# A Fourier mixing layer in front of a gated feed-forward: the 47-point transform first, the complex 64-point one second, data as matmul weights in the mixing

## The chip, the cores and the metric

The kernel runs on one core of a Trainium2 chip, in one launch. The metric is the device time of that launch in microseconds (us). The core's engines work beside each other: TensorE (PE, with its weight loads shown apart as PEld), VectorE (DVE), ScalarE (ACT), GpSimd (POOL), and SyncE (SP), which here only issues DMAs. Results of TensorE land in PSUM, everything else is in SBUF.

## The reference, cut to what matters

```
X  = np.fft.rfft(x, axis=1)                 # x: (8, 3008, 256), float32
Yr = Xr @ w_r - Xi @ w_i + b_r              # w_r, w_i: (256, 256)
Yi = Xr @ w_i + Xi @ w_r + b_i
Yr = sign(Yr) * max(|Yr| - 0.01, 0);  Yi likewise
y  = np.fft.irfft(Yr + 1j*Yi, n=3008, axis=1)
t  = y.reshape(24064, 256)
h  = t @ w_in                               # (256, 2048), float64
out = (h * cos(h)) @ w_out                  # (2048, 256), float64
```

The first six lines are called the Fourier part here, the last three the feed-forward.

## The kernel before

**The Fourier part.** 3008 = 64 * 47, and the two factors have no common divisor, so the 3008-point transform is a 64-point one along one index and a 47-point one along the other, with no twiddle factors between. It is done in three stages for each batch b, with a trip through DRAM (`scr1`, `scr2`) between them. `stage_a(b)` (lines 319 to 359) is the real 64-point transform: a fixed matrix is the weights, the data stream past it, 12 chunks of 512 columns. `stage_b(b)` (362 to 581) does four steps for 32 values of the first frequency, in four groups q of eight: `f2t1` is the 47-point transform with the data as weights, so that the result comes out with the 256 channels on the partitions; `wmix` multiplies by w_r, w_i and their sum, these as weights, and thresholds; `inverse` turns the result back with TensorE transposes (`t2`) and does the inverse 47-point transform (`idft`). `stage_c(b, t)` (586 to 645) is the inverse 64-point transform for block t of 512 tokens (six blocks t a batch, the last of 448), again with data as weights; it leaves the tokens as `xTh` and `xTl`, channels on partitions.

**The number format of the products.** Where accuracy needs it, a float32 operand is split into two float32r parts, high and low, and a product takes three matmuls (high*high, low*high, high*low). The high part is a cast, the low part a subtraction on POOL (`rest_pool`) or DVE (`rest`). For batch 0 the stages use plain float32 matmuls. The trace records a float32 matmul as two records: `f2t1` of batch 0 does four matmuls for a pair of values and shows eight.

**The feed-forward.** `moe_step(b, t, f, pull)` does one of 16 slices f of the inner 2048 for one block t: six matmuls into `ph`, then ACT and DVE make `u` = h cos h and its parts `gh`, `gl`; three slices later `second` adds six matmuls into the two `po` banks. All of these are float32r matmuls of 512 columns (448 in the last block).

**What sets the order.** In the opening, batch 0's `stage_a0` and `stage_b(0)` run with `stage_a(1)` woven in, and with them half of the splitting of w_in and w_out out of float64 (`split_f64`, sixteen pieces: eight of w_in, eight of w_out; DVE, ACT and POOL). Then the feed-forward of batch b runs block by block, and between its slices `pull` takes steps of the generator `ahead(b)`: `stage_c` of the next block, `stage_b(b+1)`, and `stage_a(b+2)` woven in. The number behind each `yield` is the cost by which `pull` meters these steps. The remaining eight pieces are split during batch 0's first block. Each engine then runs its own instructions strictly in the order in which they were laid down.

```
544            bo = stage_out("bo")[:96]
545            nc.scalar.copy(bo, p[:96])
...
547            nc.sync.dma_start(dst[:, s0:s0 + 2, :], bo.rearrange("p (s d) -> p s d", s=2))
```

Of the kernel before, what the change touches and what calls it, by code (L numbers as in the profile page):

```python
# [53 lines left out]
def _index():  # L54
    n1, n2 = np.arange(64), np.arange(48)
    return (47 * n1[None, :] + 64 * n2[:, None]) % N


def _constants():
    n1, s = np.arange(64), np.arange(32)  # L60
    ang = 2 * np.pi * (np.outer(n1, s) % 64) / 64
    f1 = np.zeros((2, 64, 2, 2, 32))
    ei = np.zeros((2, 2, 32, 2, 64))
    alt = (-1.0) ** n1
    for g in range(2):
        f1[g, :, 0, g, :] = np.cos(ang)
        f1[g, :, 1, g, :] = -np.sin(ang)
        f1[g, :, 1, g, 0] = alt
        ei[0, g, :, g, :] = np.cos(ang).T
        ei[1, g, :, g, :] = -np.sin(ang).T  # L70
        ei[1, g, 0, g, :] = alt

    f1 = f1.reshape(128, 4, 32).transpose(0, 2, 1).reshape(128, 128)
    ei = ei.reshape(128, 128) * (2.0 / N)
    crt = {(k % 64, k % 47): k for k in range(N)}
    th = 2 * np.pi * (np.outer(np.arange(47), np.arange(47)) % 47) / 47
    C, S = np.cos(th), np.sin(th)
    f2 = np.zeros((32, 2, 48, 2, 48))
    sig = np.ones((32, 48))
    for sl in range(1, 32):  # L80
        for k2 in range(47):
            sig[sl, k2] = 1 if crt[sl, k2] <= N // 2 else -1
        f2[sl, 0, :47, 0, :47] = C
        f2[sl, 1, :47, 0, :47] = S
        f2[sl, 0, :47, 1, :47] = -S * sig[sl, :47]
        f2[sl, 1, :47, 1, :47] = C * sig[sl, :47]
    i1 = np.zeros((2, 2, 48, 2, 48))
    i1[1, 0, :47, 0, :47] = C
    i1[1, 0, :47, 1, :47] = S
    i1[1, 1, :47, 0, :47] = -S  # L90
    i1[1, 1, :47, 1, :47] = C
    for r, k1 in ((0, 0), (1, 32)):
        for j in range(24):
            c = r * 24 + j
            sig[0, c] = 1 if crt[k1, j] <= N // 2 else -1
            f2[0, r, :47, 0, c] = C[:, j]
            f2[0, r, :47, 1, c] = -S[:, j] * sig[0, c]
            i1[0, 0, c, r, :47] = (0.5 if j == 0 else 1.0) * C[j]
            if j:
                i1[0, 1, c, r, :47] = -S[j]  # L100
    f2 = np.concatenate([f2, f2[:, :, :, :1] + f2[:, :, :, 1:]], 3)
    f2 = f2.reshape(32, 96, 144).transpose(1, 0, 2)

    i1 = i1.reshape(2, 96, 4, 24).transpose(1, 0, 3, 2).reshape(96, 2, 96)
    c_f1 = np.stack(_split(f1), 1)
    c_f3 = f2.astype(np.float32)
    c_f2 = np.concatenate(_split(f2[:, :, :96]), 2)
    c_i1 = np.stack(_split(i1), 1)
    c_ei = np.concatenate(_split(ei), 1)
    c_sig = np.concatenate([np.ones((48, 32)), sig.T]).astype(np.float32)  # L110
    c_ff = np.concatenate([f1, ei], 1).astype(np.float32)
    c_if = i1.astype(np.float32)
    return [np.ascontiguousarray(a) for a in (c_f1, c_f2, c_i1, c_ei, c_sig, c_f3, c_ff, c_if)]
# [3 lines left out]
def tile_body(ctx: ExitStack, tc, x, w_r, w_i, b_r, b_i, w_in, w_out,  # L117
              c_f1, c_f2, c_i1, c_ei, c_sig, c_f3, c_ff, c_if, out):
# [9 lines left out]

    ff = cp.tile([128, 256], F32, name="ff")
    nc.gpsimd.dma_start(ff, c_ff)  # L130
    f1 = cp.tile([128, 2, 128], F32R, name="f1")
    ident = cp.tile([128, 128], F32, name="ident")
    make_identity(nc, ident)
    i1 = cp.tile([96, 2, 2, 96], F32R, name="i1")
    ei = cp.tile([128, 256], F32R, name="ei")
    sig = cp.tile([96, 32], F32, name="sig")


    bb = cp.tile([128, 2, 2], F32, name="bb")
    blo = cp.tile([128, 2, 2], F32, name="blo")  # L140
    bhi = cp.tile([128, 2, 2], F32, name="bhi")
    bhn = cp.tile([128, 2, 2], F32, name="bhn")

    def load_constants():
        with nc.allow_non_contiguous_dma(reason="bias"):
            for r, bsrc in enumerate((b_r, b_i)):
                nc.gpsimd.dma_start(bb[:, r, :], bsrc.rearrange("(c p) -> p c", p=128))
        nc.gpsimd.dma_start(sig, c_sig)
        nc.gpsimd.dma_start(fi[0], c_if)

    def load_split_constants():
        nc.gpsimd.dma_start(f1, c_f1)
        nc.gpsimd.dma_start(i1, c_i1)
        nc.gpsimd.dma_start(ei, c_ei)

    def bounds():
        nc.vector.tensor_scalar(out=blo, in0=bb, scalar1=-1.0, scalar2=-LAM, op0=ALU.mult, op1=ALU.add)
        nc.vector.tensor_scalar(out=bhi, in0=bb, scalar1=-1.0, scalar2=LAM, op0=ALU.mult, op1=ALU.add)
        nc.vector.tensor_scalar(out=bhn, in0=bhi, scalar1=-1.0, scalar2=None, op0=ALU.mult)

# [5 lines left out]
    def split_w(hi, lo, src):  # L166
        nc.vector.tensor_copy(hi, src)
        nc.vector.tensor_tensor(out=lo, in0=src, in1=hi.bitcast(F32), op=ALU.subtract)

    fi, ws, f0, a0 = {}, {}, {}, {}  # L170

    def load_fourier_w():
        wr, wi, wc = (pool["pro"].tile([128, 512], F32, tag=n, name=n, bufs=1) for n in ("wr", "wi", "wc"))
        ws.update(enumerate((wr, wc, wi)))
# [3 lines left out]
    def sum_fourier_w():  # L178
        wr, wc, wi = (ws[j] for j in range(3))
        nc.vector.tensor_tensor(out=wc, in0=wi, in1=wr, op=ALU.subtract)  # L180
        nc.vector.tensor_tensor(out=wi, in0=wi, in1=wr, op=ALU.add)

    def split_fourier_w():
        for j, w in ws.items():
            split_w(wf[:, j, 0].rearrange("p c e -> p (c e)"), wf[:, j, 1].rearrange("p c e -> p (c e)"), w)
# [10 lines left out]
    def split_f64(hi, lo, raw):  # L196
# [43 lines left out]
    mm = nc.tensor.matmul  # L240

    def rest_pool(lo, x, hi):
        return nc.gpsimd.tensor_tensor(out=lo, in0=x, in1=hi.bitcast(F32), op=ALU.subtract)  # L243

    def rest(lo, x, hi):
        return nc.vector.tensor_tensor(out=lo, in0=x, in1=hi.bitcast(F32), op=ALU.subtract)  # L246

    scr1, scr2 = {}, {}

# [10 lines left out]
    def stage_in(name):  # L260
        return wk.tile([128, 512], F32, tag="xt", name=name, bufs=4)

    def stage_out(name):
        return wk.tile([128, 512], F32, tag="ao", name=name, bufs=3)

    def beside(*gens):
        gens = list(gens)
        while gens:
            for g in list(gens):
                c = next(g, None)  # L270
# [554 lines left out]
```

## Time and profile before

| | |
|---|---|
| median of 3 runs | 2763.29 us (2761.89 to 2765.01) |
| span of the profiled execution | 2764.1 us |
| PE busy | 2726.7 us, 99% of the span, 13422 matmul records |
| DVE busy | 2099.5 us, 76% |
| ACT busy | 1783.9 us, 65% |
| POOL busy | 1193.0 us, 43% |
| DMA | 174.54 MB, 63 GB/s in the mean |

The profiled execution's span lies within the three runs. A matmul's busy time in the trace is longer than the time that it holds TensorE up, since the next one starts before it has ended: a 128x512 matmul shows 0.39 us, and the next starts 0.23 us after it. So what a matmul costs is read from start to start.

### The profile page before, as it was taken

Reading aid. Unit: us, or ns where it says so; the run is one execution under the profiler, and the core shown is the slowest. Engines: PE = TensorE matmul, PEld = TensorE weight load, DVE = VectorE, ACT = ScalarE, POOL = GpSimd, SP = SyncE. Lnnn points to the kernel's source line nnn. Section 1 sums busy time; section 2 is a strip of 40 time slices with the busy share of each in tenths; the row PEclk is TensorE's granted clock in tenths of the full one; section 3 lists DMA queues with packets and bytes.
Section 4 is the critical chain, followed back from the end, with each engine's and each line's share of the span. In section 5 each row is a group of like instructions: output and inputs, shape, how many; then the busy total and the mean of one; then the engine's idle time right before and its main releaser. Section 6 shows DMA issues by size and latency. Waiting matters only on the chain.

```text
span 2764.1 us, 39129 instructions
## 1 busy us (share of the span) xinstructions
PE 2726.7 (99%) x13422; PEld 2312.3 (84%) x13422; DVE 2099.5 (76%) x3754; ACT 1783.9 (65%) x3480; POOL 1193.0 (43%) x1017
## 2 busy tenths in 40 slices
PE   8889999999999999999999999999999999999999
PEld 6568888888888888888888888888888888888888
DVE  5698776778778787787877878688777777766665
ACT  5565666666666666666666666666666666666666
POOL 4454543444434454344443544345442444333222
PEclk9899999999999999999999999999999999999999
DMA  7411222122211221212212122121221111010000
GB/s 213 142 56 56 82 68 67 53 70 70 66 61 47 72 81 52 74 51 71 76 46 75 55 74 72 48 72 58 71 76 62 44 48 56 24 58 23 9 16 15
DMA packets 113415, 174.54 MB, mean 63 GB/s; under 512 B 11169, under 2 KB 60177, under 8 KB 113217
## 3 DMA queue, kind: packets, MB, share of 16 engines
q1 hardware_dynamic: 104064, 146.51, 16.9%
q0 software_dynamic: 9152, 25.54, 3.4%
q8 instruction: 106, 1.74, 0.3%
q14 instruction: 93, 0.75, 0.1%
HBM read 100.18 MB, written 71.83 MB: 62 GB/s over the span
## 4 chain that ended last, share of the span: by engine, by line
PE 91%; DVE 1%; issue 0%; ACT 0%; DMA 0%; POOL 0%; ACTq 0%; SPq 0%; DVEq 0%
PE ph L676 12%; PE ph L678 12%; PE ph L677 12%; PE po L658 12%; PE po L659 12%; PE po L662 12%; PE pi L542 3%; PE pw L474 2%; PE pw L476 2%; PE pw L475 2%; PE pb L436 2%; PE pc L635 2%; PE pt L509 2%; PE pb L438 1%; PE pc L636 1%; PE pa L353 1%
## 5 line engine op out<-in xcount | busy, mean ns | idle before, releaser
L243 POOL TENSOR_TENSOR gl<-u,gh 128x512 fp32r<-128x512 f32 (+1 forms) x384 | 493.4, 1285 | 913.3 <-ACT gh L688 654.1
L684 DVE SCALAR_TENSOR_TENSOR u<-ph,u 128x512 f32<-128x512 f32 (+1 forms) x768 | 518.2, 675 | 247.3 <-ACT u L683 243.0
L687 DVE TENSOR_TENSOR u<-ph,u 128x512 f32<-128x512 f32 (+1 forms) x768 | 519.0, 676 | 221.1 <-ACT u L686 208.6
L686 ACT ACTIVATE u<-u 128x512 f32<-128x512 f32 (+1 forms) x768 | 479.6, 625 | 305.0 <-DVE u L684 301.5
L683 ACT ACTIVATE u<-ph 128x512 int32<-128x512 f32 (+1 forms) x768 | 450.9, 587 | 272.7 <-PE ph L678 244.4
L676 PE MATMUL ph<-xTh,win 128*128 128x512 f32 (+1 forms) x1536 | 600.9, 392 | 1.6 <-DVE u L687 1.4
L678 PE MATMUL ph<-xTh,win 128*128 128x512 f32 (+1 forms) x1536 | 600.0, 391 | 0.0
L659 PE MATMUL po<-gh,wout 128*128 128x512 f32 (+1 forms) x1536 | 596.6, 389 | 1.8 <-DVE wout L216 1.8
L677 PE MATMUL ph<-xTl,win 128*128 128x512 f32 (+1 forms) x1536 | 597.5, 389 | 0.6 <-DVE xTl L644 0.6
L658 PE MATMUL po<-gh,wout 128*128 128x512 f32 (+1 forms) x1536 | 596.9, 389 | 1.2 <-ACT wout L214 0.9
L688 ACT CAST gh<-u 128x512 fp32r<-128x512 f32 (+1 forms) x768 | 468.4, 610 | 191.5 <-DVE u L687 182.0
L662 PE MATMUL po<-gl,wout 128*128 128x512 f32 (+1 forms) x1536 | 482.5, 389 | 2.8 <-DVE gl L246 2.8
L246 DVE TENSOR_TENSOR gl<-u,gh 128x512 fp32r<-128x512 f32 (+1 forms) x384 | 330.8, 861 | 32.0 <-ACT gh L688 25.5
L658 PEld LDWEIGHTS po<-gh,wout 128*128 128x128 f32 x1536 | 288.6, 188 | 54.9 <-ACT wout L214 1.3
L676 PEld LDWEIGHTS ph<-xTh,win 128*128 128x128 f32 x1536 | 289.6, 189 | 53.1 <-DVE u L687 3.6
L678 PEld LDWEIGHTS ph<-xTh,win 128*128 128x128 f32 x1536 | 289.4, 188 | 52.7
L659 PEld LDWEIGHTS po<-gh,wout 128*128 128x128 f32 x1536 | 288.5, 188 | 53.2 <-DVE wout L216 2.3
L677 PEld LDWEIGHTS ph<-xTl,win 128*128 128x128 f32 x1536 | 289.7, 189 | 51.1 <-DVE xTl L644 1.0
L662 PEld LDWEIGHTS po<-gl,wout 128*128 128x128 f32 x1536 | 284.4, 188 | 54.9 <-DVE gl L246 3.9
L243 POOL TENSOR_TENSOR al<-at,ah 96x512 fp32r<-96x512 f32 x112 | 148.8, 1329 | 168.7 <-PE pb L438 53.7
L243 POOL TENSOR_TENSOR bl<-bt,bh 128x512 fp32r<-128x512 f32 x94 | 124.6, 1325 | 218.5 <-PE pa L355 66.2
L528 DVE SCALAR_TENSOR_TENSOR yl<-pt,sig,yh 96x256 fp32r<-96x256 f32 x224 | 103.8, 474 | 28.1 <-ACT yh L527 26.9
(127 smaller groups left out, 3631.2 us busy)
## 6 DMA issues: line engine op xcount, KB each, us to landing
scr<-bo SPq DMA_DIRECT2D x128, 192.0 KB, 2.1
bt<-scr SPq DMA_DIRECT2D x96, 256.0 KB, 2.8
xt<-in_dram SPq DMA_DIRECT2D x84, 256.0 KB, 2.9
scr<-ao SPq DMA_DIRECT2D x84, 256.0 KB, 2.0
at<-scr SPq DMA_DIRECT2D x112, 192.0 KB, 2.5
out_dram<-ob SPq DMA_DIRECT2D x80, 256.0 KB, 2.2
f<-in_dram POOLq DMA_DIRECT2D x56, 288.0 KB, 3.3
raw<-in_dram POOLq DMA_DIRECT2D x16, 512.0 KB, 6.8
```

The lines of the kernel that those rows point to most:

```text
L243: return nc.gpsimd.tensor_tensor(out=lo, in0=x, in1=hi.bitcast(F32), op=ALU.subtract)
L658: mm(po[e][:, :n], wo[0][:, 0, f, es], gh[:, :n], start=f == 0, stop=False)
L659: mm(po[e][:, :n], wo[0][:, 1, f, es], gh[:, :n], start=False, stop=False)
L662: mm(po[e][:, :n], wo[0][:, 0, f, es], gl[:, :n], start=False, stop=f == NFC - 1)
L676: mm(h, win[:, 0, c, fs], th[:, c, :n], start=c == 0, stop=False)
L677: mm(h, win[:, 0, c, fs], tl[:, c, :n], start=False, stop=False)
L678: mm(h, win[:, 1, c, fs], th[:, c, :n], start=False, stop=c == 1)
L683: nc.scalar.activation(k[:, :n], h, AF.Identity, bias=0.25, scale=1.0 / TWO_PI)
L684: nc.vector.scalar_tensor_tensor(out=u[:, :n], in0=h, scalar=1.0 / TWO_PI, in1=k[:, :n], op0=ALU.mult, op1=ALU.subtract)
L686: nc.scalar.activation(u[:, :n], u[:, :n], AF.Sin, bias=HALF_PI, scale=TWO_PI)
L687: nc.vector.tensor_tensor(out=u[:, :n], in0=h, in1=u[:, :n], op=ALU.mult)
L688: nc.scalar.copy(gh[:, :n], u[:, :n])
```

## The change

The transform is done in the other order, and the layout between the steps follows from that. Per batch:

- `stage_a` is the real 47-point transform (24 frequencies): 96 partitions, 16 chunks of 512 columns instead of 12. Batches 2 and up in float32r parts, batch 0 and 1 in float32, as before.
- `stage_b` works in `NP` = 12 groups m of two values of the 47-point frequency. `fwd(m)` is a complex 64-point transform with the data as weights, now in plain float32: four matmuls of 128 columns. `wmix(m)` takes the transformed data as weights and streams w_r, -(w_r+w_i) and w_i-w_r past them: three products of six float32r matmuls of 256 columns. The result stands with frequencies on partitions, so nothing is transposed. `idft(m)` is the inverse 64-point transform: three float32r matmuls of 512 columns. `fwd(m)`, `wmix(m-1)` and `idft(m-2)` follow each other.
- `stage_c` is the inverse 47-point transform with data as weights, in plain float32: 16 units u a batch, four matmuls of 94 columns each; a unit gives 188 tokens, so units straddle the blocks of 512. The tiles `xTh` and `xTl` get three buffers instead of two.
- The bias is added from a tile broadcast over partitions, the threshold uses constants, and the sign flips are folded into a tile `sig`.
- Batch 0 goes through the same `fwd`, `wmix` and `idft` as the others; only its input comes by transposes from `a0` (48 instead of 64). So the split parts of w_r and w_i (`wf`) are made at the start (`fourier_w`), before the first `wmix`.
- The pieces of w_in are split within the first 60 woven steps instead of 80; `stage_a(1)` gets a step after every four steps of `stage_b(0)` instead of seven.
- Rings: `xp` 8 tiles instead of 6, `xt` 5 instead of 4, `ao` 4 instead of 3; the metered costs are new.

```diff
     def stage_a(b):
-        for c in range(12):
+        for c in range(16):
...
-                mm(p, f1[:, 0], xh, start=True, stop=False)
-                mm(p, f1[:, 1], xh, start=False, stop=False)
-                mm(p, f1[:, 0], xl, start=False, stop=True)
+                mm(p, fas[:, 0], xh, start=True, stop=False)
+                mm(p, fas[:, 1], xh, start=False, stop=False)
+                mm(p, fas[:, 0], xl, start=False, stop=True)
...
+        def fwd(m):
...
+            for k in range(2):
+                for c in range(2):
+                    o = 256 * k + 128 * c
+                    mm(pv[:, c, k], a[:, o:o + 128], f2[:, 2 * (m % 2) + k], start=o == 0, stop=o == 384,
+                       skip_group_check=True)
...
+            nc.scalar.copy(xr, p[:, :256])
+            nc.vector.tensor_tensor(out=xs, in0=p[:, 256:], in1=xr, op=ALU.add)
+            nc.scalar.copy(hv, p)
+            nc.vector.tensor_tensor(out=lv, in0=p, in1=hv.bitcast(F32), op=ALU.subtract)
+            nc.scalar.copy(hs, xs)
+            rest_pool(ls, xs, hs)
...
+        def wmix(m):
...
+                for c in range(2):
+                    mm(p, xh[:, comp, c], wf[:, j, 0, c], start=first and c == 0, stop=False, skip_group_check=True)
+                    mm(p, xh[:, comp, c], wf[:, j, 1, c], start=False, stop=False, skip_group_check=True)
+                    mm(p, xl[:, comp, c], wf[:, j, 0, c], start=False, stop=stop and c == 1, skip_group_check=True)
...
+            nc.vector.tensor_scalar(out=cl, in0=z, scalar1=-LAM, scalar2=LAM, op0=ALU.max, op1=ALU.min)
+            nc.gpsimd.tensor_tensor(out=z, in0=z, in1=cl, op=ALU.subtract)
...
+            nc.scalar.copy(yh, z)
+            rest_pool(yl, z, yh)
...
+        def idft(m):
...
+            for n, (h, y) in enumerate(((0, yh), (1, yh), (0, yl))):
+                for lo, hi, v in parts:
+                    mm(p[:, lo:hi], inv[:, h, v], y[:, lo:hi], start=n == 0 and lo == 0, stop=n == 2 and hi == 512,
+                       skip_group_check=True)
...
     def stage_c(b, t):
-                    mm(p[:, 256 * c:256 * c + 256], bh[:, j, cs], ei, start=c == 0, stop=False, skip_group_check=True)
-                    mm(p[:, 256 * c:256 * c + 128], bl[:, j, cs], ei[:, :128], start=False, stop=c == 1,
-                       skip_group_check=True)
+                    mm(p[:, o:o + 94], bt[:, j, 128 * c:128 * c + 128], last, start=j == c == 0, stop=j == c == 1,
+                       skip_group_check=True)
```

How the instructions now stand, at two places. In these rows a program's matmul of float32 is one row, not two. First TensorE in the first batch of the feed-forward, where the Fourier part is laid between the slices. Before, with `pi` the inverse transform and `pt` the transposes:

```order
L676 MATMUL ph<-xTh,win 128x512
L542 MATMUL pi<-yh,i_74 96x512 x2
L677 MATMUL ph<-xTl,win 128x512
L542 MATMUL pi<-yl,i_74 96x512
L509 MATMUL pt<-ident,st 96x128 x4
L678 MATMUL ph<-xTh,win 128x512
```

And now, with the mixing (L361 to L363) that has `Xh` and `Xl` as weights, between the slices' matmuls (L495 to L497):

```order
L495 MATMUL ph<-xTh,win 128x512
L496 MATMUL ph<-xTl,win 128x512
L497 MATMUL ph<-xTh,win 128x512
L363 MATMUL p_2060<-wf,Xl 128x256
L361 MATMUL p_2060<-wf,Xh 128x256
L362 MATMUL p_2060<-wf,Xh 128x256
```

The transposes are gone there, and the slices' own matmuls stand between the groups as they did.

Second VectorE at the end of the opening, where the first slice of the feed-forward begins. Before, from the second piece of w_out that VectorE finishes (L216) to the first `u` (L684); L603, L626, L643 and L644 belong to `stage_c`:

```order
L216 TENSOR_TENSOR wout<-wa,wq 128x512
L603 CAST bh<-bt 128x512
L206 TENSOR_SCALAR wm<-wm 128x512
L626 TENSOR_TENSOR xTl<-pc,xTh 128x2x128
L207 TENSOR_SCALAR wq<-wm 128x512
L209 SCALAR_TENSOR_TENSOR wa<-raw,wq 128x512
L603 CAST bh<-bt 128x512
L643 TENSOR_TENSOR tc<-pc,xTh 128x256
L211 TENSOR_SCALAR wq<-wa 128x512
L643 TENSOR_TENSOR tc<-pc,xTh 128x256
L644 TENSOR_TENSOR xTl<-pc,tc 128x2x128 x2
L684 SCALAR_TENSOR_TENSOR u<-ph,u 128x512 x2
```

And now, from the last rows of the opening's `stage_c` (L462) on; L186 finishes a piece, and the one shown is the sixth of w_out, L503 and L506 make `u`:

```order
L462 TENSOR_TENSOR xTl<-pc,xTh 128x2x136
L181 TENSOR_SCALAR wq<-wa 128x512
L462 TENSOR_TENSOR xTl<-pc,xTh 128x2x52
L462 TENSOR_TENSOR xTl<-pc,xTh 128x2x188 x2
L186 TENSOR_TENSOR wout<-wa,wq 128x512
L176 TENSOR_SCALAR wm<-wm 128x512
L177 TENSOR_SCALAR wq<-wm 128x512
L179 SCALAR_TENSOR_TENSOR wa<-raw,wq 128x512
L181 TENSOR_SCALAR wq<-wa 128x512
L503 SCALAR_TENSOR_TENSOR u<-ph,u 128x512
```

Before, two pieces of w_out are finished ahead of the first `u` and six behind it; now six stand ahead of it and two behind. On GpSimd three of w_out's pieces (two instructions each) now stand ahead of the last `yl` of `stage_b(0)`; before, all of them stood behind the last subtraction of that stage.

## Rows read from the trace of the kernel before

**Rows 1.** The page: busy time, share of the span, instructions of TensorE.

```profile
PE 2726.7 (99%) x13422; PEld 2312.3 (84%) x13422; DVE 2099.5 (76%) x3754; ACT 1783.9 (65%) x3480; POOL 1193.0 (43%) x1017
```

**Rows 2.** The page: engines' shares of the chain that ended last.

```profile
PE 91%; DVE 1%; issue 0%; ACT 0%; DMA 0%; POOL 0%; ACTq 0%; SPq 0%; DVEq 0%
```

**Rows 3.** Busy us by engine (x instructions) in one window, then PE clock, DMA share.

```profile
131.07:240.00 108.93, 97.73 (x435) 78.61 (x435) 99.37 (x153) 67.19 (x127) 60.09 (x52) 0.96 0.19 59
```

**Rows 4.** The chain's longest pieces in order of time: start, us, what; one batch apart.

```profile
932.08 0.94 PE pi L542 x4
...
1267.68 0.94 PE pi L542 x4
```

**Rows 5.** Timeline of TensorE: start, us, line, operands; 512 columns in float32r.

```profile
1000.39 0.39 PE L678 MATMUL ph<-xTh,win 128*128 128x512 f32 x1
...
1002.66 0.63 PE L542 MATMUL pi<-yh,i 96*96 96x512 f32 x2
...
1003.36 0.34 PE L474 MATMUL pw<-Xh,wf 128*128 128x384 f32 x1
```

**Rows 6.** The same: twelve matmuls of the mixing lie between these two.

```profile
938.27 0.33 PE L474 MATMUL pw<-Xh,wf 128*128 128x384 f32 x1
...
940.37 0.39 PE L659 MATMUL po<-gh,wout 128*128 128x512 f32 x1
```

**Rows 7.** The same: the 47-point transform, data as weights; two pairs.

```profile
2239.30 0.32 PE L436 MATMUL pb<-f,ah 96*128 96x192 f32 x1
...
2239.74 0.32 PE L436 MATMUL pb<-f,ah 96*128 96x192 f32 x1
```

**Rows 8.** The same: the inverse 64-point transform, data as weights; a pair.

```profile
423.61 0.34 PE L635 MATMUL pc<-ei,bh 128*128 128x256 f32 x1
423.78 0.22 PE L636 MATMUL pc<-ei,bl 128*128 128x128 f32 x1
423.84 0.34 PE L635 MATMUL pc<-ei,bh 128*128 128x256 f32 x1
```

**Rows 9.** The same, in the opening: float32, and transposes.

```profile
43.01 1.15 PE L428 MATMUL pb<-f,at 96*128 96x144 f32 x8
43.99 0.27 PE L376 MATMUL pq<-ident,a 128*96 128x128 f32 x1
...
97.50 1.25 PE L509 MATMUL pt<-ident,st 128*96 128x128 f32 x10
98.59 1.02 PE L350 MATMUL pa<-xt,ff 128*128 128x512 f32 x2
99.46 0.81 PE L470 MATMUL pw<-Xf,wr 128*128 128x384 f32 x2
```

**Rows 10.** The same: from the first of five 256-column matmuls, 96-column weights.

```profile
917.88 0.51 PE L542 MATMUL pi<-yh,i 96*96 96x256 f32 x3
...
918.47 0.40 PE L353 MATMUL pa<-xh,f 128*128 128x512 f32 x1
```

**Rows 11.** The same: start and end of stage_b(0), start of the feed-forward.

```profile
20.81 1.05 PE L376 MATMUL pq<-ident,a 128*96 128x128 f32 x8 [1.62 <-DVE a L316]
...
113.94 1.88 PE L538 MATMUL pi<-yf,fi 96*96 96x512 f32 x4
...
131.07 1.48 PE L676 MATMUL ph<-xTh,win 128*128 128x512 f32 x3
```

**Rows 12.** Timeline of GpSimd in the opening.

```profile
16.00 0.18 POOL L289 COPY seen<-x 128x1 f32<-128x1 f32 x1 [10.96 <-DMA wr<-in_dram]
...
29.13 1.29 POOL L213 TENSOR_TENSOR wq<-wm,wq 128x512 f32<-128x512 f32 x1
...
65.78 2.42 POOL L492 TENSOR_TENSOR st<-st,cl 128x384 f32<-128x384 f32 x1 [2.68 <-ACT st L491]
69.63 1.00 POOL L497 TENSOR_TENSOR st<-st,cl 128x384 f32<-128x384 f32 x1 [1.43 <-DVE cl L495]
```

**Rows 13.** Groups of GpSimd: count, busy us, mean ns, idle before.

```profile
L193 POOL DMA_DIRECT2D raw<-in_dram x16 | 11.3, 707 | 43.3 <-ACT bo L545 20.4 <-DVE wq L211 7.0 <-issue 5.3
```

More of the change, by code (lines that the diff above doesn't have):

```diff
@@ L112, in _constants @@
-    c_if = i1.astype(np.float32)
-    return [np.ascontiguousarray(a) for a in (c_f1, c_f2, c_i1, c_ei, c_sig, c_f3, c_ff, c_if)]
+    fb = np.zeros((2, 64, 24, 2, 64))
+    for c in range(24):
+        fb[0, :, c, 0] = C
+        fb[1, :, c, 0] = S
+        fb[0, :, c, 1] = -S * sign[None, :, c]
+        fb[1, :, c, 1] = C * sign[None, :, c]
+    fb = fb.reshape(128, 24, 128)
+    w = np.where((n1 == 0) | (n1 == 32), 1.0, np.where(n1 < 32, 2.0, 0.0))[:, None]
+    inv = np.zeros((2, 2, 64, 64, 2))
@@ L238, in moe_w @@
             yield
[L240 to L248, printed above, removed]
+    scr1, scr2, a0 = {}, {}, {}
     banks = []
@@ L562, in stage_b @@
+        load(0)
+        load(1)
         turn(0)
         yield 2.5
[L564 to L579 removed]
@@ L580, in stage_b, with tokens @@
-        yield 2.0
-        yield from inverse(3)
+        for m in range(NP + 2):
+            if m < NP:
+                turn(m + 1)
+                load(m + 2)
+                yield from fwd(m)
+            if 1 <= m <= NP:
+                yield from wmix(m - 1)
+            if m >= 2:
+                yield from idft(m - 2)
     xT = {}
+    def tokens(b, t):
+        if (b, t) not in xT:
+            xT[b, t] = tuple(pool["mo"].tile([128, 2, 512], F32R, tag=n, name=n, bufs=3) for n in ("xTh", "xTl"))
+        return xT[b, t]
@@ new lines, in load @@
+        def load(u):
+            if u < hi:
+                ld[u] = stage_in("bt")[:96].rearrange("p (j d) -> p j d", j=2)
+                nc.sync.dma_start(ld[u], scr2[b][2 * u:2 * u + 2].rearrange("j g r k d -> (g r k) j d"))
+        load(lo)
+        load(lo + 1)
+        yield 2.5
+        for u in range(lo, hi):
+            if u > lo:
+                load(u + 1)
+            bt = ld.pop(u)
+            p = fps("pc")
+            for j in range(2):
+                for c in range(2):
+                    o = 188 * c + 94 * j
+                    mm(p[:, o:o + 94], bt[:, j, 128 * c:128 * c + 128], last, start=j == c == 0, stop=j == c == 1,
+                       skip_group_check=True)
+                if j == 0:
+                    yield 0.43
+            pv = p[:, :376].rearrange("p (c n) -> p c n", c=2)
+            at = 188 * u
+            while at < 188 * u + 188:
+                end = min(188 * u + 188, 512 * (at // 512 + 1))
+                th, tl = (v[:, :, at % 512:at % 512 + end - at] for v in tokens(b, at // 512))
+                src = pv[:, :, at - 188 * u:end - 188 * u]
+                nc.scalar.copy(th, src)
+                nc.vector.tensor_tensor(out=tl, in0=src, in1=th.bitcast(F32), op=ALU.subtract)
+                at = end
+            yield 0.43
@@ L708, in tile_body @@
         warm(WARM)
-        fi[0] = pool["pro"].tile([96, 2, 96], F32, name="fi", bufs=1)
         stage_a0()
         load_constants()
+        fw = fourier_w()
+        next(fw)
         early = 0
@@ L776, in tile_body @@
             open_ = [True]
[L777 removed]
+            rate = (c_cost(b, t) + share(b, t)) / (NFC - 1) / 2
             def pull():
```

566 lines of the change are left out of this document (167 added, 399 removed).

## The prediction

> **What bounds the kernel now.** I read the busy times first: TensorE is busy for 99% of the span, DVE for 76%, ACT and POOL for less [rows 1]. Then the chain of work that ended last: 91% of it lies on TensorE and 1% on the next engine [rows 2]. Third, how regular that is: the same step of the inverse transform stands on the chain at 932.08 and at 1267.68 [rows 4], so a batch in the middle takes 335.6 us, with no idle row on TensorE in between. So from about 240 us on the kernel is a sum of TensorE's start-to-start prices, and the question is what the new matmuls cost there. Before that it is not: B(0), my name for `stage_b` of batch 0, runs from 20.81 to about 115.8, the feed-forward starts at 131.07 [rows 11], and from there to 240 TensorE is idle for 108.9 - 97.7 = 11.2 us while DVE is busy for 99.4, with a PE clock of 0.96 [rows 3]. That stretch is DVE's.
>
> **Prices, start to start.** 512 columns in float32r: ten from 1000.39 to 1002.66, 0.227 each; with 96-column weights three in 0.70, 0.233 each [rows 5]. 384 columns: twelve in 2.10, 0.175 [rows 6]. Transposes: ten in 1.09, 0.109; a float32 record of 512 columns: two in 0.87, 0.435; of 144 columns: eight in 0.98, 0.1225 [rows 9], so 128 columns in proportion 0.109. A pair of 192 and 96 columns with data as weights: 0.22 [rows 7]. This last one matters most: 288 columns streamed at the slope of 384 to 512 columns, 0.0004 us a column, would take 0.12, and the pair takes 0.22. So a matmul with new 128-column weights cannot go below about 0.11, however few columns it streams. The pair of 256 and 128 columns takes 0.23 [rows 8]; less 0.11 for the short one, 0.12 for 256 columns, and the run of five with 96-column weights says 0.118 [rows 10].
>
> **The steady part, edit by edit.** The feed-forward keeps its matmuls, 96 slices of 12 a batch: 1152 x 0.227, the last block in proportion, 256 us. The Fourier part now (first number) and then:
> - `stage_b`, 7 batches behind the opening. Now: 64 pairs x 0.22 = 14.1; mixing 144 x 0.175 = 25.2; 64 transposes x 0.109 = 7.0; inverse 45 x 0.233 + 6 x 0.118 = 11.2; together 57.5. Check: 57.5 + 8.2 for `stage_a` + 48 x 0.23 = 11.0 for `stage_c` + 256 = 333, measured 335.6. Then: `fwd` 48 float32 matmuls, 96 records x 0.11 = 10.6; mixing 216 x 0.12 = 25.9; inverse 33 x 0.227 + 6 x 0.12 = 8.2; together 44.7. The transposes and the padding of the inverse go, the mixing costs what it did, since 256 columns stream for 0.12. 7 x (44.7 - 57.5) = -89.6.
> - `stage_a`, 6 batches: 36 x 0.227 = 8.2, then 48 x 0.233 = 11.2: +18.0.
> - `stage_c`: 376 pairs x 0.23 = 86.5 (the first block apart). Then 125 units of four float32 matmuls, 1000 records: 94 columns stream for 0.1225 x 94/144 = 0.08, but each has new 128-column weights, so 0.11: 110. +23.5. Bounds 80 and 112, I take the floor of rows 7, since that row has the same kind of operand.
>
> Sum -48.1. The other engines get less to do there (DVE's split of data before each transform and its two-step subtractions go; the longest new chain, mixing to inverse, is two groups of m deep, with a batch's slices between), so nothing hides the gain again: DVE was at 76% without stopping TensorE.
>
> The Trainium skill, page TensorE: Matmul & The Clock Gate, section LDWEIGHTS, says that a weight load takes the columns over 1.2 GHz, and that fewer rows don't shorten it. That speaks against `stage_c` here: its load is full although it has 96 rows and streams 94 columns. It makes an estimate of 0.107 us a load, and 107 instead of 110 for `stage_c`; the trace agrees with 0.11 [rows 7].
>
> **The opening.** Now, 95 us for B(0) with `stage_a(1)`. TensorE's sum then: 48 transposes 5.2, `fwd` 10.6, mixing 25.9, inverse 8.2, `stage_a(1)` 32 records x 0.435 = 13.9; 64 us. That would end at 85 to 96. But POOL becomes longer: the two subtractions of each group are its own now. A 128x512 subtraction takes 1.29 [rows 12], a 256 one I put at 0.7 (estimate, half of it). 12 groups x (2 x 1.3 + 0.7) = 40; the order puts eleven pieces of w_in and w_out ahead of the last `yl`, 11 x 2 x 1.3 = 29; `wf` 4 x 1.3 = 5; 21 DMA issues at 0.55 to 0.707 [rows 13], 12 to 15. Sum 86 to 89 behind 16.00, where its first work starts [rows 12]: 102 to 105 if it never waits, and it did wait often before. So the opening ends between 103 (gain 12) and, with 20 us of waits, 123 (loss 7). I take 110, nearer to the sum: -6. The way from there to the first slice, 15 us now (DRAM and `stage_c`), stays: 12 matmuls instead of 16, but eight more of the next block's stand ahead of the slice.
>
> From 131 to 240 the loss was 11.2 us of idling, and about 0.04 x 109 = 4 for the clock. DVE's order has six pieces of w_out ahead of the first `u` instead of two, so two of six are left in its way. I take 4/6 of 15: -9; bounds 0 and -15.
>
> Sum: -48 - 6 - 9 = -63. 2764.1 - 63 = 2701; the profiled execution lies 0.8 above the median, so **2700**.
>
> **Rivals.**
> 1. `stage_c` isn't bound by its loads: 1000 x 0.08 instead of 0.11, -30 more: 2670. For it: rows 7 is float32r, and no warm float32 row with so few columns exists. Against: the transposes and the 128-column price coincide with the floor and so don't contradict it.
> 2. The opening is lost to GpSimd. A subtraction of 384 columns took 1.00 once and 2.42 another time, with DVE at work on SBUF [rows 12]. If a third of the 24 new subtractions takes 1.4 more, POOL's sum grows by 11, and `yl` is late for each inverse: opening +10 instead of -6, 2716. If all do, +34: 2740. The Trainium skill, page SBUF — State Buffer, section Who interferes with whom, says that DVE and GpSimd share a pair of ports, which one locks for a whole instruction. The row of 2.42 agrees with a wait of that size; it doesn't show the cause.
> 3. **Slower**: in the mixing a 256-column matmul holds TensorE not for 0.12 but for what rows 8 show behind one, 423.61 to 423.78, 0.17. 1512 such matmuls x 0.05 = +76: 2776. It decides at 0.12 + 63/1512 = 0.162. For it: the row, and that each has new 128-column data as weights, 216 in a row of groups. Against: the short one behind it takes 0.06, less than its own load, so the pair shares its time out; and five 256s in a row take 0.118 [rows 10], though with 96-column weights.
> 4. The change doesn't do what it says, and TensorE starts to wait between slices: at the idle share of 131 to 240, a tenth, the whole gain would be gone in 630 us. The order shows the transposes gone and the slices where they were. Against it too: each group's loads have two groups of work ahead of them. 2764 or so.
>
> **How the numbers follow.** The forecast 0.72, rival 1 0.07, rival 2 0.14, rival 3 0.04, rival 4 0.03. The forecast's own range takes the bounds of the opening (-12 to +7), of the start of the feed-forward (-15 to 0) and 0.005 us on each mixing matmul (8 us): 2680 to 2722. Rival 1 lies partly below. Range 2674 to 2722. A measurement of this kernel tells about 0.2% from no change, 5.5 us. Faster 0.94 (the forecast, rivals 1 and 2, and part of 4), same 0.02, slower 0.04.
>
> **What would show it.** The time between equal steps of two batches should fall from 335.6 to 329 (by 76.7 - 70.0). Mixing runs should start 0.12 apart, `stage_c`'s records 0.11, `fwd`'s 0.11, no transposes in the middle. The feed-forward should start between 118 and 138, with GpSimd the busiest engine or close to it in the opening, and TensorE's idle time in the 109 us behind it should be well below 11. Wrong would be: mixing at 0.16 or more; idle rows on TensorE behind 250 us; a batch above 333.

## The result, and the profile after

The changed kernel takes 2729.3 us (median; 2727.9 to 2731.1) beside 2763.0 for the one before in the same session: ratio 0.9875, 95% interval 0.9861 to 0.9889. It is faster, but by 34 us and not by the 63 of the forecast, and 2729.3 lies 7 us above the range. The two profiled executions differ by 2764.1 - 2726.7 = 37.4 us of span.

The page of the changed kernel: engines' busy time, which answers [rows 1], and the chain that ended last, which answers [rows 2].

```profile
PE 2680.1 (98%) x13551; PEld 2292.9 (84%) x13551; DVE 1836.5 (67%) x3144; ACT 1760.8 (65%) x3323; POOL 1027.3 (38%) x882
...
PE 94%; DVE 1%; DMA 1%; issue 0%; ACT 0%; POOL 0%; ACTq 0%; POOLq 0%; DVEq 0%
```

The chain of the changed kernel in the middle (start, us, what): the same step one batch apart, and a run of `stage_c`.

```profile
866.96 0.89 PE pb L337 x8
...
881.48 1.31 PE pc L451 x12
...
1196.05 0.89 PE pb L337 x8
```

Its timeline of TensorE: six mixing matmuls lie between the first and the last of these rows.

```profile
902.92 0.28 PE L361 MATMUL p<-wf,Xh 128*128 128x256 f32 x1
...
903.52 0.28 PE L363 MATMUL p<-wf,Xl 128*128 128x256 f32 x1
903.63 0.40 PE L495 MATMUL ph<-xTh,win 128*128 128x512 f32 x1
```

A batch takes 1196.05 - 866.96 = 329.1 us, where it took 335.6 [rows 4]. The mixing costs 0.71 / 6 = 0.118 apart, `fwd` 0.89 / 8 = 0.111 a record, `stage_c` 1.31 / 12 = 0.109. These are the prices of the forecast. The loss is in the opening. Its timeline on TensorE, which answers [rows 11]: `stage_a0` (line 254), the first transposes of B(0) (323), its last inverse (401), the first slice of the feed-forward (495); in brackets what TensorE waited for.

```profile
6.99 27.62 PE L254 MATMUL pa<-fa,x 96*128 96x96 f32 x128 [2.17 <-DMA fa<-in_dram]
39.81 2.79 PE L323 MATMUL pq<-ident,a 128*128 128x128 f32 x12 [5.20 <-ACT a L256]
...
140.01 0.79 PE L401 MATMUL pi<-yl,inv 128*128 128x512 f32 x1 [0.15 <-POOL yl L139]
149.32 8.81 PE L451 MATMUL pc<-last,bt 96*128 96x94 f32 x40 [8.52 <-DMA bt<-scr]
157.85 1.63 PE L495 MATMUL ph<-xTh,win 128*128 128x512 f32 x3
```

B(0) starts at 39.8 instead of 20.8, and the feed-forward at 157.85 instead of 131.07: 26.8 us later, where I expected it between 118 and 138. The windows of the changed kernel (busy us of PE, PEld, DVE, ACT, POOL with their counts, PE clock, DMA share, GB/s) show a DVE that is nearly full inside B(0), and almost no idle TensorE behind the start; the last row answers [rows 3].

```profile
50.00:80.00 30.00, 25.70 (x151) 20.47 (x150) 27.34 (x55) 18.87 (x41) 20.96 (x19) 0.89 0.31 96
80.00:110.00 30.00, 23.71 (x139) 18.60 (x137) 28.64 (x50) 15.97 (x34) 24.05 (x22) 0.94 0.48 144
...
157.85:240.00 82.15, 80.80 (x384) 67.51 (x384) 60.96 (x102) 56.48 (x106) 34.49 (x29) 0.97 0.18 56
```

ACT's timeline before the feed-forward shows what its queue held: operations of the w_out pieces (lines 175 and 182) that wait for raw loads, and the last `bo` and `xTh` copies between them.

```profile
141.07 0.58 ACT L404 COPY bo<-pi 128x512 f32<-128x512 f32 x1
146.21 0.66 ACT L175 ACTIVATE wm<-raw 128x512 f32<-128x512 f32 x1 [4.57 <-DMA raw<-in_dram]
147.82 0.67 ACT L182 ACTIVATE wm<-raw 128x512 f32<-128x512 uint32 x1 [0.95 <-DVE wq L177]
151.35 0.47 ACT L461 CAST xTh<-pc 128x376 fp32r<-128x376 f32 x1 [2.18 <-PE pc L451]
154.41 0.67 ACT L175 ACTIVATE wm<-raw 128x512 f32<-128x512 f32 x1 [2.58 <-DMA raw<-in_dram]
154.97 0.74 ACT L461 CAST xTh<-pc 128x376 fp32r<-128x376 f32 x2
```

So my first theory was Q: each engine takes its work in order, `stage_a0`'s copies and B(0)'s last copies stand behind pieces, and another order gets the time back.

### The profile page after: what moved, and what is told of

The parts are those of the page before. It is cut to its first block, busy times and chain, and to the rows that moved or that the text cites. A ratio compares the mean times of both kernels' runs of the same rounds, so it can differ in the third digit from the quotient of the medians.

```text
span 2726.7 us, 38048 instructions
## 1 busy us (share of the span) xinstructions
PE 2680.1 (98%) x13551; PEld 2292.9 (84%) x13551; DVE 1836.5 (67%) x3144; ACT 1760.8 (65%) x3323; POOL 1027.3 (38%) x882
## 4 chain that ended last, share of the span: by engine, by line
PE 94%; DVE 1%; DMA 1%; issue 0%; ACT 0%; POOL 0%; ACTq 0%; POOLq 0%; DVEq 0%
PE ph L495 13%; PE po L477 13%; PE po L478 13%; PE po L481 13%; PE ph L496 13%; PE ph L497 13%; PE pc L451 4%; PE pb L337 3%; PE p L363 2%; PE p L362 2%; PE p L361 2%; PE pi L401 2%; PE pa L295 1%; PE pa L293 1%; PE pa L294 1%; DMA raw<-in_dram 1%
## 5 line engine op out<-in xcount | busy, mean ns | idle before, releaser
L503 DVE SCALAR_TENSOR_TENSOR u<-ph,u 128x512 f32<-128x512 f32 (+1 forms) x768 | 520.2, 677 | 322.3 <-ACT u L502 316.4
L506 DVE TENSOR_TENSOR u<-ph,u 128x512 f32<-128x512 f32 (+1 forms) x768 | 521.6, 679 | 304.4 <-ACT u L505 288.6
L495 PE MATMUL ph<-xTh,win 128*128 128x512 f32 (+1 forms) x1536 | 613.5, 400 | 1.3 <-DVE u L506 1.3
L497 PE MATMUL ph<-xTh,win 128*128 128x512 f32 (+1 forms) x1536 | 595.4, 388 | 0.0
L481 PE MATMUL po<-gl,wout 128*128 128x512 f32 (+1 forms) x1536 | 473.3, 388 | 0.0
L497 PEld LDWEIGHTS ph<-xTh,win 128*128 128x128 f32 x1536 | 289.3, 188 | 55.9
L142 DVE TENSOR_TENSOR gl<-u,gh 128x512 fp32r<-128x512 f32 (+1 forms) x384 | 288.6, 752 | 67.6 <-ACT gh L507 64.6
L495 PEld LDWEIGHTS ph<-xTh,win 128*128 128x128 f32 x1536 | 290.6, 189 | 47.5 <-DVE u L506 1.9
L496 PEld LDWEIGHTS ph<-xTl,win 128*128 128x128 f32 x1536 | 290.4, 189 | 44.8
L387 POOL TENSOR_TENSOR z<-z,cl 128x512 f32<-128x512 f32 x96 | 129.4, 1348 | 243.4 <-DVE cl L386 243.4
L139 POOL TENSOR_TENSOR xl<-xt,xh 96x512 fp32r<-96x512 f32 x96 | 127.0, 1323 | 179.2 <-DVE xh L275 110.1
L451 PEld LDWEIGHTS pc<-last,bt 96*128 96x128 f32 x1024 | 151.6, 197 | 22.8 <-issue 9.0
```

What stands on the lines that cost most here:

```text
L481: mm(po[e][:, :n], wo[0][:, 0, f, es], gl[:, :n], start=False, stop=f == NFC - 1)
L495: mm(h, win[:, 0, c, fs], th[:, c, :n], start=c == 0, stop=False)
L496: mm(h, win[:, 0, c, fs], tl[:, c, :n], start=False, stop=False)
L497: mm(h, win[:, 1, c, fs], th[:, c, :n], start=False, stop=c == 1)
L503: nc.vector.scalar_tensor_tensor(out=u[:, :n], in0=h, scalar=1.0 / TWO_PI, in1=k[:, :n], op0=ALU.mult, op1=ALU.subtract)
L506: nc.vector.tensor_tensor(out=u[:, :n], in0=h, in1=u[:, :n], op=ALU.mult)
```

## Experiments

"Pieces" are the sixteen parts of w_in and w_out that `split_f64` loads and splits. All times are of kernels made from the changed one, which takes 2729.3, unless said otherwise. The runs that leave work out were timed once each, the others four times. The start of the feed-forward is the first matmul of its first slice, in the profiled execution.

**Three orders.** The first run:

```diff
-            mark["a0"] = (nc.vector.tensor_copy if n % 2 else nc.scalar.copy)(
+            mark["a0", n % 2] = (nc.vector.tensor_copy if n % 2 else nc.scalar.copy)(
...
-                next(fw)
+                with behind(("a0", 0), ("a0", 1)):
+                    next(fw)
...
-                next(mw, None)
+                with behind(("a0", 0), ("a0", 1)):
+                    next(mw, None)
```

`behind` lets what stands inside it be taken up only after the marked instructions, here the last two copies of `stage_a0`.

> The changed kernel, but ACT and DVE may take up the splitting of the Fourier weights and of the w_in pieces only after the last PSUM copy of stage_a0. Theory Q (in-order queues: A0's copies stand behind piece work that waits for raw loads): B(0)'s first transposes start at 22 to 27 us instead of 39.81, the matmuls of stage_a0 run gapless, and since some of the piece work comes back inside B(0) the feed-forward starts 5 to 15 us earlier than 157.85; total 2714 to 2724 us. Rival W (DVE simply has that much work before the feed-forward, wherever it stands): B(0) starts early but ends no earlier, feed-forward start 154 to 160, total 2726 to 2733. Rival X (96-partition loads land late and hold stage_a0): B(0) still starts after 34 us.

2729.8 us. B(0) began at 34.87, 5 us earlier but still after 34, as rival X had it (what held `stage_a0` is read in the last section). The last inverse of B(0) ended at 143.7 instead of 140.8 and the feed-forward began at 160.29: nothing ended earlier, as rival W said. The second run gates the w_out pieces in `moe_w` by the last copies of `stage_c(0,0)` in the same way.

> The changed kernel, but ACT and DVE may take up the w_out pieces only after the last copy of stage_c(0,0). Theory Q: the last bo copy and stage_c's xTh copies no longer stand behind operations that wait for raw loads; the feed-forward starts at 138 to 148 us instead of 157.85, and the first product with w_out comes later, with 4 to 8 us of TensorE idle behind the start; total 2718 to 2725. Rival P (what is moved is paid back whole, since each piece still holds 3.2 us of DVE ahead of the first products): the start is earlier but the stretch from it to batch 1 grows by as much; total 2726 to 2733.

2728.7 us. The feed-forward began at 140.88, 17 us earlier, and lost it behind: windows of this run,

```profile
160.00:200.00 40.00, 32.02 (x155) 25.86 (x155) 39.29 (x63) 28.28 (x55) 22.31 (x21) 0.96 0.22 65
200.00:240.00 40.00, 35.88 (x177) 29.20 (x176) 38.32 (x58) 27.29 (x51) 27.17 (x22) 0.99 0.37 108
```

TensorE idles for 8.0 + 4.1 us while DVE is busy for 77.6 of 80. Rival P was right.

> Both orders together. Theory Q: the two effects add; feed-forward start 122 to 138, total 2703 to 2717. Rival W/P: total 2724 to 2733.

2738.0 us: worse, and outside both ranges. Theory Q falls as to the time: none of these orders got time back. The first two only moved the place where the pieces are paid, and the two together cost 9 us more; why is not shown.

**Without the pieces**, in both kernels (the weights are zero):

```diff
     def moe_w():
-        for k in range(16):
...
+        return iter(())
```

> The changed kernel without the 16 pieces of w_in and w_out: neither loaded nor split, the two weight tiles are set to zero once, so the feed-forward multiplies by zeros. It shows the opening with B(0) alone. Theory Q (the pieces' order is the loss): feed-forward start 105 to 122 us. Rival R (the new B(0) is itself the longer one, by its four quarter operations for z and the chain through DVE and GpSimd): feed-forward start above 135.

> The kernel before without the 16 pieces of w_in and w_out (not loaded, not split; the two weight tiles are zero). The changed kernel without them started its feed-forward at 127.5 us. Theory D (DVE's work, stretched where GpSimd works beside it, sets the length of the new opening; the pieces cost the new one more than the old): the old opening without pieces is 5 to 15 us shorter than with them, feed-forward start 116 to 126, so that the pieces cost 30 us in the new opening and 5 to 15 in the old. Rival Q (the new opening is longer by its stages, whatever the pieces): feed-forward start 100 to 108, the same 27 us ahead of the changed kernel as with pieces.

2695.9 us, and 2734.0 for the kernel before (2764.3 with pieces in that session). The new start, 127.50, lies between theory Q (105 to 122) and rival R (above 135). Timelines of TensorE, `stage_a0`, B(0)'s start and end, and the first slice: the changed kernel without pieces,

```profile
6.24 27.62 PE L250 MATMUL pa<-fa,x 96*128 96x96 f32 x128 [1.42 <-DMA fa<-in_dram]
34.60 2.79 PE L319 MATMUL pq<-ident,a 128*128 128x128 f32 x12 [0.74 <-DVE a L252]
...
112.59 0.50 PE L397 MATMUL pi<-yl,inv 128*128 128x512 f32 x1 [0.73 <-POOL yl L139]
127.50 1.63 PE L491 MATMUL ph<-xTh,win 128*128 128x512 f32 x3
```

and the kernel before without pieces.

```profile
6.51 13.08 PE L309 MATMUL pa<-ff,x 128*128 128x128 f32 x96 [1.69 <-DMA ff<-in_dram]
21.21 1.05 PE L371 MATMUL pq<-ident,a 128*96 128x128 f32 x8 [1.62 <-DVE a L311]
...
105.48 1.88 PE L533 MATMUL pi<-yf,fi 96*96 96x512 f32 x4
...
118.89 0.91 PE L671 MATMUL ph<-xTh,win 128*128 128x512 f32 x3
```

The last output copies of batch 0 on ACT, in the order before, changed, before without pieces, changed without pieces (one row of each kernel):

```profile
488.04 0.97 ACT L666 COPY ob<-po 128x448 f32<-128x448 f32 x2 [1.39 <-PE po L662]
```

```profile
495.42 0.97 ACT L485 COPY ob<-po 128x448 f32<-128x448 f32 x2
```

```profile
456.28 0.97 ACT L661 COPY ob<-po 128x448 f32<-128x448 f32 x2
```

```profile
463.13 0.97 ACT L481 COPY ob<-po 128x448 f32<-128x448 f32 x2
```

This is the account of the miss. Up to the end of batch 0 the pieces cost 488.04 - 456.28 = 31.8 us in the old kernel and 495.42 - 463.13 = 32.3 in the new. Ahead of the feed-forward they cost 12.2 and 30.3; the rest lies behind it. So 18 us of the late start are a shift and no loss, and batch 0 ends 7 us later with or without pieces. Theory D's start (116 to 126) came true, but its reading, that the pieces cost the new kernel more, holds for the start alone and not for the time. Half the pieces:

> The changed kernel with the eight w_in pieces only: the w_out pieces are neither loaded nor split, that weight tile is set to zero. Without any piece the kernel took 2695.9, with all sixteen 2729.3, so the pieces cost 33. Theory J (every piece costs about the same 2 us wherever it stands, because DVE, ACT and GpSimd all have no room in the opening): 2711 to 2716, feed-forward from 140 to 145. Rival S (the w_out pieces, which stand around the end of the first batch, cost nearly all of it): 2696 to 2702, feed-forward from 128 to 132. Rival I (the w_in pieces in the middle of B(0) cost nearly all): 2723 to 2729.

> The changed kernel with the eight w_out pieces only (the tile of w_in is zero). Theory J: 2711 to 2716. Rival S: 2723 to 2729, feed-forward after 148. Rival I: 2696 to 2702.

2714.7 and 2712.2: 18.8 and 16.3 us above no pieces, together 35 where all cost 33. That is theory J in the totals: either half costs about 2 us a piece. The start with the w_in pieces alone, 146.36, lies just above J's 140 to 145, and single pieces were not taken out.

**A part of each piece's work left out.** First lines 176 and 181 on DVE, then line 183 and the subtraction on GpSimd:

> The changed kernel with two of the five DVE operations of each piece left out (the clamp of line 176 and the mask of line 181; the low parts of the weights come out otherwise). Loads, ACT's and GpSimd's operations stay. In the changed kernel these two took 10.6 + 7.9 = 18.5 us of DVE ahead of the feed-forward. Theory D: the feed-forward starts 10 to 20 us earlier, 138 to 148. Rival Q (raw loads that come one after another, and the queues behind them, set the length): 154 to 160.

> The changed kernel with both GpSimd operations of each piece left out (the product of line 183 and the subtraction for the low part; the low parts come out otherwise). DVE's own instructions all stay. Theory D with its second half (GpSimd stretches those DVE operations that read and write SBUF alone): line 176 takes 0.42 to 0.5 us at the median instead of 0.78, DVE's busy time ahead of the feed-forward falls from 111 to 92 to 100 us, the feed-forward starts at 138 to 148. If DVE's operations are stretched by something else: their durations stay, start 150 to 158.

2722.0 and 2715.8 us, starts at 152.53 and 142.92. Up to the start DVE was busy for 96.2 us in the first run and for 96.1 in the second, instead of 108.5. In the first the start moved by 5.3; neither theory's numbers hold. In the second line 176 fell from 788 to 501 ns in the mean and the start moved by 15, as theory D said. With the same time on DVE the two starts lie 10 us apart, so the amount of DVE's work alone does not set the start. Groups of DVE up to the start (count, busy us, mean ns, idle): the changed kernel,

```profile
L176 DVE TENSOR_SCALAR wm<-wm 128x512 f32<-128x512 f32 x14 | 11.0, 788 | 18.5 <-ACT wm L175 18.4
...
L379 DVE TENSOR_TENSOR z<-p,k 64x256 f32<-64x256 f32 x24 | 10.0, 418 | 3.5 <-POOL wa L139 2.3 <-issue 0.5 <-PE p L363 0.4
```

and without GpSimd's part of the pieces.

```profile
L176 DVE TENSOR_SCALAR wm<-wm 128x512 f32<-128x512 f32 x14 | 7.0, 501 | 16.1 <-ACT wm L175 15.9
```

**DVE relieved in B(0)** (its copies of the transposes and its clamps given to ACT):

```diff
-                (nc.vector.tensor_copy if m % 2 else nc.scalar.copy)(at[m], p)
+                nc.scalar.copy(at[m], p)
...
-            nc.vector.tensor_scalar(out=cl, in0=z, scalar1=-LAM, scalar2=LAM, op0=ALU.max, op1=ALU.min)
+            if b == 0:
+                nc.scalar.activation(cl, z, AF.Relu, bias=-LAM, scale=-1.0)
+                nc.scalar.activation(z, z, AF.Relu, bias=-LAM)
...
```

> The changed kernel with DVE relieved in B(0) alone: all twelve copies of the transposes on ACT (they were split between the two), and the threshold of B(0) as two Relu on ACT and the subtraction on GpSimd in place of a clamp on DVE and the subtraction. DVE loses 6 x 0.68 = 4.1 and 12 clamps that took 9.0 us, ACT gains about 3.5 + 12 x 1.2 = 18. Theory D: feed-forward 8 to 13 us earlier, total 2716 to 2722. Rival (ACT's queue, with its waits for raw loads, is as much the bound): total 2726 to 2738.

> Both edits: stage_a0 filled up, DVE relieved in B(0). Theory A: 2703 to 2712. Theory D: as the run with DVE relieved alone, within 3 us.

2729.5 and 2729.9 us, the rival's number. Up to the start DVE was busy for 101.1 us instead of 108.5, ACT for 92.0 instead of 76.2, and the time did not move. TensorE's wait for ACT's `yh` in B(0) grew from 11.3 to 15.0 us. Theory D's numbers fall; but the edit also loads ACT, so it does not show that DVE has time to spare.

**stage_a0 filled up.** Its 128 records stand 27.62 / 128 = 0.21 us apart, twice the 0.109 of `stage_c`'s records of nearly the same shape (96 rows, 94 columns). Filled with zeros to 128 rows and 128 columns:

```diff
-                    mm(p[:, o:o + 96], xs[n // 2][:, k:k + 128], fa, start=o == 0, stop=o == 288,
+                    mm(p[:, o:o + 128], xs[n // 2][:, k:k + 128], fa, start=o == 0, stop=o == 384,
...
```

> The changed kernel with the matmuls of stage_a0 filled up by zeros to 128 rows and 128 columns (the form that the kernel before had there); PSUM copies take the same columns as now. The 128 records of line 254 stand 0.213 us apart over all of stage_a0, those of the kernel before, with full tiles, came to 0.10 to 0.11. If the small tiles are what keeps TensorE at the lower price: 0.11 to 0.15 each, stage_a0 ends with the loads at 21 to 25 us instead of 38. If not: 0.21 still. For the time, theory D: the feed-forward starts 0 to 5 us earlier and the total is 2724 to 2730, since DVE has its work still to do; rival C (the late start of B(0) is passed on whole): start 143 to 147, total 2714 to 2720.

2734.5 us, outside both ranges: the fills delayed the constant, and the first matmul came at 12.23. B(0) began at 38.81, only 1 us earlier. With the zeros inside the constant:

> The changed kernel without the pieces (weights zero, as in the run before without them), and with the matmuls of stage_a0 filled up with zeros to 128 rows and 128 columns; the zeros come with the loaded constant and by eight fills of 32 partitions ahead of the loads, so that nothing delays the first matmul. Without the filling stage_a0's records stood 0.213 us apart, B(0) began at 34.6 and the feed-forward at 127.5. Theory T (the small tiles keep TensorE at its lower price, and this is the 13 us by which the new opening starts late): 0.10 to 0.15 each, B(0) from 21 to 25, feed-forward from 114 to 119, total 2682 to 2688. Rival: 0.213 still, everything as without the filling, 2693 to 2698. Second rival: stage_a0 gets fast, but B(0) ends no earlier, since something else in it sets its end: feed-forward 124 to 128.

2683.2 us without pieces, 12.7 less than without the filling. TensorE's timeline:

```profile
6.83 17.20 PE L253 MATMUL pa<-fa,x 128*128 128x128 f32 x128 [2.01 <-DMA fa<-in_dram]
24.77 1.50 PE L322 MATMUL pq<-ident,a 128*128 128x128 f32 x12 [0.74 <-ACT wf L155]
```

The same 128 records take 17.2 us instead of 27.6, and the feed-forward starts at 115.80: theory T, with all its numbers. The 17.2 us are not one price: the records stand 0.213 us apart at first here too, and 0.112 from 12.5 us on (last section).

> The changed kernel with the same filling of stage_a0, with all pieces. Theory A (the prices of the opening add up: late start of B(0), and pieces): feed-forward 10 to 13 us earlier than 157.85, total 2715 to 2721. Theory D (DVE and GpSimd, which wait for each other, have the pieces' and B(0)'s work to do, and TensorE's time in stage_a0 lies beside it): total 2725 to 2733.

2732.2 us: with all pieces it gives nothing, although B(0) starts at 29.35. That is theory D's number; the run does not show its cause. Here the pieces cost 2732.2 - 2683.2 = 49.0 us, where they cost 33 without the filling: the two prices do not add up.

**Two raw buffers** (`bufs=2`, u and ao one fewer), the order with two w_out pieces ahead of `stage_c(0,0)` as in the old kernel, and both with `stage_a0` filled up. Of the four runs here the first has the buffers alone, the second both, the third the order alone, the fourth everything:

> The changed kernel with two raw buffers for the eight w_out pieces instead of one (to make room: three buffers for u instead of four, three for ao instead of four). In the changed kernel the last operations of these pieces end 9.2 us apart (117.8 to 182.3), in the kernel before 12.1 (119.6 to 204.2). Theory S (a chain of load, two readings by ACT, release, next load, one after another, holds ACT's queue and with it the last bo and xTh copies): the pieces stand 5 to 7 us apart, ACT's waits for raw loads ahead of the feed-forward shrink from 18 to under 8 us, the feed-forward starts at 143 to 153, total 2715 to 2723. Rival D (the pieces' own work on DVE and GpSimd, which wait for each other, sets the distance): 8 to 9.5 us still, total 2726 to 2733.

> Two raw buffers, and from the third w_out piece on ACT and DVE take a piece up only after the last copy of stage_c(0,0), so that two pieces stand ahead of it as in the kernel before. Theory S: feed-forward at 130 to 142, TensorE idle between it and 240 for 0 to 5 us, total 2708 to 2719. Rival D: the start is early, idle time behind it 10 or more, total 2724 to 2730.

> One raw buffer as in the changed kernel, the order of the run before (two w_out pieces ahead of stage_c(0,0), six behind). Theory S: feed-forward at 138 to 146, the pieces still 9 to 11 us apart, so idle behind the start 5 to 12 us, total 2721 to 2729. It tells what the order alone is worth.

> Two raw buffers, that order, and stage_a0 filled up to 128 rows and columns. Theory S with theory A (what held the feed-forward was the pieces' chain, and without it the 10 us of stage_a0 count): 5 to 12 us under the run without the filling. Theory D: within 3 us of it.

2729.6, 2730.5, 2728.8 and 2723.3 us. With two buffers the w_out pieces came 7.5 us apart instead of 9.2, between the two theories, and it was worth nothing; the feed-forward started at 163.68, and with the order as well at 152.02. Theory S falls. With the order alone the start was at 150.72 and TensorE idled for 5.8 us between it and 240. Only the last is better: ratio to the kernel before 0.9849 (0.9835 to 0.9864), 7.1 us less than the run without the filling, in the 5 to 12 that theories S and A gave for this difference. It is the fastest kernel with all the work in it.

## Why the prediction was wrong

- **The steady part, -48: right.** From the last outputs of batch 0 to the end, spans less starts of those rows: 2276.1 before, 2231.3 after, -44.8, where the forecast had -48.1 + 6.5 = -41.6. The block of batch 0, read without pieces from its first slice to those outputs, went from 337.4 to 335.6, -1.8 instead of -6.5. Together -46.6, where the forecast had -48.1. Rivals 1 (`stage_c` below its loads) and 3 (mixing at 0.162 or more) are answered by 0.109 and 0.118, rival 4 by a chain without idle rows.
- **The opening, -6: the waits were mis-sized.** The forecast's end of 110 was for a B(0) with its pieces: GpSimd's work of 86 to 89 us behind 16.00, and up to 20 us of waits. It ended at 140.80. GpSimd's work in that stretch is what was added up, 89.0 us, but it was idle for 35.8, the late start of B(0) included (columns as in the windows above):

```profile
16.00:140.80 124.80, 95.92 (x519) 78.20 (x518) 100.27 (x180) 67.96 (x138) 89.03 (x84) 0.91 0.49 148
```

With the pieces B(0) went from 95.0 to 101.0 us. Without them it went from 107.36 - 21.21 = 86.2 to 113.09 - 34.60 = 78.5, and the way to the first slice from 11.5 to 14.4: -4.8. That this is near -6 is luck, since the forecast did not take the pieces out.
- **The start of B(0): the missing term.** My sum began at 16.00 with GpSimd and left the start at 20.8. `stage_a0` changed too, to 96 rows and columns, and I gave it no price. Its records stood 0.213 us apart for 27 us, at TensorE's lower clock level, and not 0.11 (last section). It costs +13.4 without pieces (34.60 - 21.21), and the filled run takes 12.7 us of that away. With all pieces the filling is worth 7.1 in one arrangement and nothing in another.
- **The idle time behind the start, -9: the step that failed by its reasoning.** (4/6 of 15 is 10, not 9.) "Two of six are left in its way" was true of the place: the idle fell from 11.2 us to 1.35. But I booked the four pieces that moved ahead as free. Their price only moved: 31.8 us before and 32.3 now. The term is 0.5, not -9.

The four terms: -46.6 - 4.8 + 13.4 + 0.5 = -37.5; the spans differ by 37.4. The terms are differences of the same four traces, so this sum closes by itself. Its division does not: with `stage_a0` filled up the pieces cost 49.0 us and not 32.3, so how much of the 14 us belongs to `stage_a0` and how much to the pieces depends on which is taken out first. The last 3.7 us to the medians lie in which executions were profiled: a time is about 2 us above its span (2764.25 and 2762.1 in a run of the kernel before), so the one profiled before took about 2766 us, an estimate, more than the four timed ones.

The upper end of the range takes the 8 us on the mixing downward only. Taken both ways it would be 2730 and would have held the result, but by luck, since the mixing cost what the forecast said.

Rival 2 named times from 2716 to 2740 (its 11 and 34 us counted from an opening without the gain of 6), and the result lies there. But its mechanism is not what was found: GpSimd's subtractions of 512 columns in B(0) and for the pieces took 1.27 to 1.41 us in the mean, and it is DVE that waits. DVE was also the fuller of the two: 28.6 us of 30 in one stretch, and 108.5 up to the first slice beside 99.7 on GpSimd.

Open is what keeps the pieces from being hidden. It is not one order, not the distance of the loads, not DVE's amount of work alone: taking two DVE operations out of each piece gave 7 us, taking GpSimd's two gave 14, taking all gave 33. That B(0) is a chain through ACT, DVE and GpSimd in which every inserted operation delays the next one fits the runs, and is argued, not shown.

## What to carry to other kernels

Where one-off work has to be done ahead of the steady part, an order that moves it out of one stretch puts it into another; price it by leaving it out of both kernels before booking a gain. Price every stage that changes shape, the first one too, and by rows of its own shape and place. A stage that gets faster ahead of a stretch with no room (here `stage_a0`) may show its gain only once the rest is taken away. And before a clock column is believed at the start of a trace, compare the distance of matmuls of a known price.

## What the runs showed of the hardware

`stage_a0` ran at the lower of TensorE's two clock levels (1.2 and 2.4 GHz). The run with DVE relieved shows the same records, float32 with 96 rows and 96 columns, at both levels (stretch and its length in us; busy time and number of the records and of their weight loads; granted clock; DMA share; GB/s):

```profile
6.80:8.30 1.50, 1.50 (x15) 1.50 (x15) 1.00 1.03 237
8.50:10.00 1.50, 1.50 (x9) 1.50 (x9) 0.50 1.03 257
```

Their starts lie 0.112 us apart in the first stretch and 0.213 in the second. The engine had run seven 512-column matmuls before; the clock fell while these small records ran without a gap, and it rose again at 42.5 us, in B(0). In the changed kernel's own trace the column reads 1.00 over all of `stage_a0`:

```profile
14.00:18.00 4.00, 4.00 (x21) 4.00 (x20) 1.00 1.01 242
```

But the distance is 0.213 there, and the first clock record of that trace begins at 43.56 us; where there is none, the column shows 1.00. At 43.6 us the distance falls to 0.11. In the run without pieces and with full tiles the fall lies inside `stage_a0`, at 12.5 us:

```profile
8.00:12.00 4.00, 4.00 (x21) 4.00 (x20) 1.00 1.03 254
14.00:18.00 4.00, 4.00 (x38) 4.00 (x38) 1.00 1.05 312
```

In all thirteen kernels with 96 rows and columns there, the last records of `stage_a0` stood 0.213 us apart, and the distance halved only in B(0), whose transposes have 128 of both. In the five that were filled up and the two with the old stages it halved inside `stage_a0`, between 10.1 and 17.4 us, and the last records stood 0.112 apart. So what the filling changed is when the clock rose. Whether rows or columns decide wasn't tried.

DVE operations on SBUF alone wait for GpSimd's. Timelines of the changed kernel, DVE and then GpSimd:

```profile
89.65 0.98 DVE L382 SCALAR_TENSOR_TENSOR z<-p,sig,k 64x256 f32<-64x256 f32 x2
90.67 1.74 DVE L186 TENSOR_TENSOR win<-wa,wq 128x512 fp32r<-128x512 f32 x1
92.44 0.69 DVE L179 SCALAR_TENSOR_TENSOR wa<-raw,wq 128x512 uint32<-128x512 uint32 x1
```

```profile
90.58 1.28 POOL L139 TENSOR_TENSOR yl<-z,yh 128x512 fp32r<-128x512 f32 x1 [1.43 <-ACT yh L390]
```

Line 186 takes 0.68 us at its shortest; here it takes 1.74 and lasts until 92.41, about 0.55 behind the end of GpSimd's operation at 91.86. The operations with an input in PSUM kept their price (418 ns for line 379 above, 419 without GpSimd's part of the pieces). The Trainium skill, page SBUF — State Buffer, section Who interferes with whom, says that when a DVE operation needs the ports that the two engines share, the second of the two to issue blocks until the first is done; line 186 reads two operands from SBUF, and these rows agree. What I had not expected is the direction: DVE, the fuller engine, is the one that waits.
